# One attention-and-feed-forward kernel: normaliser steps taken from GpSimd to VectorE but for the power, single fillers, token groups of three tiles, and a new order for all engines

## Chip, cores, metric

The kernel runs on one core of one Trainium2 chip, as one program. The metric is the device time of one execution in microseconds (us). A core has five engines with queues of their own that are served in order: TensorE (PE, matmuls), VectorE (DVE), ScalarE (ACT), GpSimd (POOL) and SyncE (SP), which here does nothing but issue DMAs. TensorE runs at one of two clocks, 1.2 or 2.4 GHz; the profile shows which was granted as 0.5 or 1.0.

## What is computed

Three layers, one after the other. First a gated linear attention (2 batches x 8 heads, 768 steps, head size 40), which the reference writes as a recurrence:

```
m_new = max(f + m, i);  f_stab = exp(f + m - m_new);  i_stab = exp(i - m_new)
C = f_stab * C + i_stab * v k^T;   n = f_stab * n + i_stab * k
y = sigmoid(o_gate) * (C q) / max(|n.q|, 1)
```

Its output, 1536 tokens by 320, goes through `rms = sqrt(mean(x*x) + 1e-6); xn = x / rms * rms_g`, then `(silu(xn @ w_gate) * (xn @ w_val)) @ w_out` with 1536 inner columns, then `leaky_relu(x @ w_in, 0.01) @ w_out` with 2048. Everything is float32.

## The kernel before

**Tiles.** The 1536 tokens are 12 tiles of 128 (tile T is chunk T//2 of batch T%2). The attention goes tile by tile: `qk` (scores of q and k), `arg` and `mask` (the exponents), `p` (their product), `av` and `inn` (the output within the chunk and from the state), `kv`, `st`, `cb`, `c` (the state C of that batch, which the tile after next needs), then the normaliser: `abs`, `rec`, `y1`, `yr`, `sq`, `y2`, `xn`, `xc`, and at the end `tp`, `xh`, `xl`, which transpose the tile and write it into X as a high and a low part. All large matmuls take such pairs, so that two or three matmuls stand for one float32 matmul.

**Feed-forward.** `U.g.f.h` is one up projection: 8 matmuls of 128 inner columns f (gate for h = 0, value for h = 1) over the tokens of group g. `T`, `E`, `M`, `S`, `L` make the activation and its two parts (T and S on ScalarE, the others on VectorE), `D` and `DW` project down. For f below 8 the groups are those of `GA`, for the rest those of `GB` (four tiles each). `H`, `R`, `S`, `L`, `O` are the same for the last layer. A U over a group can start when the X of all its tiles is written.

**Weights** come as 64-bit words in chunks (`wA`, `wR`, `wB` load; `a`, `r`, `b` are the four steps that convert one chunk on VectorE and ScalarE; `x` copies part of it into place by DMA).

**Order.** Nothing is scheduled by a tool: the long string `ORDER` (line 41) names every step once, `play` (line 743) issues them in that order, and each engine's queue holds its own steps in that order. An engine whose next step has to wait holds everything behind it. `id.n` (`busy`, line 173) puts n matmuls of constants into TensorE's queue; they depend on nothing and their result is never read. `att_av` adds small ones (128x184) for tiles 0 and 1 by `FILL`.

**The steps that the change touches.** `att_y2` (line 427) turns the sum of squares of a tile into 1/rms: one scale-and-add, a power of -0.5 on 128x1, and three steps of one Newton iteration, all five on GpSimd (lines 431 to 436). GpSimd also adds the mask (`att_mask`, line 310), scales the state and keys (`att_c`, `att_k`) and multiplies `eb` by q (`att_eq`, line 314).

Of the kernel before, what the change touches and what calls it, by code (L numbers as in the profile page):

```python
# [43 lines left out]
cl wA.0 a.0 id.2 dq.0 a.0 a.0 a.0 id.8 ms did dfg dig wB.0 sf.0.1 wR.1 sa.0.1 sf.1.2 sa.1.2 dmk sf.2.6 sa.2.6 eg.2.6  # L44
ex.2.6 uv.0.1 wR.0 ug.2.6 dn.0 ux.2.6 co.0.0.1 cv.0.0.1 fa.0 arg.0.0 r.1 id.2 dA.0.2 ev.1.2 wA.1 a.1 uv.1.2 fa.1
arg.0.1 qk.0 p.0.1 ex.1.2 co.1.2.6 cv.1.2.6 dsl id.2 a.1 ux.0.1 co.1.0.1 cv.1.0.1 th.0 da.2 mask.2.1 k.0 wB.1 mask.2.0
co.0.1.2 p.0.0 ux.1.2 da.1 arg.1.0 r.1 r.1 arg.1.1 a.1 a.1 co.1.1.2 av.0.0 av.0.1 kv.0 r.1 wA.3 b.0 cv.1.1.2 co.0.2.6
b.1 b.0 dr.2.6 b.0 b.0 dE.1.2 dE.2.6 r.0 dq.2 qk.2 dn.2 th.2 cv.0.1.2 dq.1 qk.1 r.0 r.0 dA.2.6 dn.1 k.1 wA.2 abs.0 b.1
arg.2.0 p.2.0 b.1 b.1 da.3 r.0 st.0 k.2 a.2 rec.0 de.2 y1.0 a.2 a.2 dr.1.2 id.9 wR.3 a.3 dn.3 p.1.0 mask.3.1 p.1.1
av.1.0 av.1.1 abs.1 kv.1 th.1 eq.2 arg.2.1 y1.1 id.7 yr.0 sq.0 a.3 rec.1 yr.1 mask.3.0 arg.3.0 x.1 p.2.1 av.2.0 av.2.1  # L50
sq.1 cb.0 dgb y2.0 xn.0 xc.0 a.3 id.2 wR.2 id.2 inn.2 wA.4 y2.1 abs.2 xn.1 xc.1 kv.2 tp.1 arg.3.1 dc.1.2 a.3 st.1 dq.3
qk.3 da.4 a.4 dq.4 y1.2 rec.2 yr.2 sq.2 a.4 y2.2 th.3 tp.0 xh.0 k.3 dv.1.2 a.2 mask.4.1 p.3.0 av.3.0 p.3.1 wB.2 cb.1
av.3.1 de.3 eq.3 cv.0.2.6 mask.4.0 dn.4 k.4 da.5 x.0 c.3 xh.1 xl.1 arg.4.1 mask.5.1 c.2 qk.4 de.4 eq.4 xl.0 a.4 r.2
U.0.1.1 U.0.1.0 T.0.1 E.0.1 M.0.1 a.4 inn.3 kv.3 dq.5 y1.3 dc.2.6 abs.3 arg.4.0 dv.2.6 xn.2 xc.2 U.0.0.0 T.0.0 E.0.0
arg.5.1 tp.2 xh.2 p.4.1 U.0.0.1 wB.3 p.4.0 S.0.1 M.0.0 S.0.0 b.2 st.3 qk.5 da.7 id.1 b.2 b.2 b.2 av.4.0 av.4.1 inn.4
th.4 mask.5.0 arg.5.0 rec.3 mask.7.1 yr.3 sq.3 xl.2 L.0.0 x.3 x.2 dn.5 p.5.1 y1.4 y2.3 id.1 U.0.3.0 T.0.3 E.0.3 c.4
p.5.0 dq.6 xn.3 abs.4 rec.4 yr.4 xc.3 sq.4 y2.4 kv.4 dn.6 k.6 id.2 de.5 L.0.1 U.0.2.0 tp.3 r.2 eq.5 xh.3 cb.3 c.5
T.0.2 b.3 U.0.3.1 M.0.3 qk.6 wA.5 st.4 cb.4 b.3 E.0.2 r.2 b.3 k.5 xn.4 xl.3 xc.4 arg.7.1 U.0.2.1 tp.4 xh.4 S.0.3 dq.7
da.6 av.5.0 av.5.1 inn.5 wB.4 M.0.2 S.0.2 L.0.2 de.6 th.5 xl.4 r.2 abs.5 x.4 a.5 wR.4 kv.5 y1.5 a.5 U.1.1.0 a.5 rec.5
L.0.3 dn.7 b.3 T.1.1 E.1.1 U.1.0.0 T.1.0 E.1.0 mask.6.0 arg.6.0 p.6.0 D.0.0.0 mask.6.1 arg.6.1 p.6.1 th.6 mask.7.0  # L60
arg.7.0 eq.6 U.1.1.1 U.1.0.1 th.7 M.1.0 st.5 K.0.0.0 D.0.0.2 K.0.0.2 wA.7 a.5 b.4 b.4 S.1.0 k.7 da.8 x.5 r.4 L.1.0 r.4
av.6.0 U.1.2.0 mask.8.1 b.4 b.4 c.6 r.3 yr.5 dq.10 av.6.1 wB.6 r.4 r.4 r.3 M.1.1 D.0.0.1 K.0.0.1 inn.6 kv.6 st.6 T.1.2
qk.7 cb.5 c.7 y1.6 U.1.2.1 mask.8.0 sq.5 de.7 y2.5 E.1.2 M.1.2 p.7.0 p.7.1 U.1.3.1 xn.5 eq.7 S.1.2 L.1.2 dn.10 r.3 r.3
S.1.1 arg.8.0 L.1.1 U.1.3.0 T.1.3 E.1.3 M.1.3 S.1.3 av.7.0 dq.8 av.7.1 U.0.5.0 T.0.5 E.0.5 inn.7 U.0.5.1 da.10
mask.10.1 cb.6 abs.7 b.6 dn.8 M.0.5 de.8 arg.10.1 U.0.4.0 L.1.3 D.1.0.1 K.1.0.1 U.0.4.1 S.0.5 k.8 T.0.4 b.6 b.6 b.6
arg.8.1 D.1.0.0 wB.7 mask.10.0 E.0.4 abs.6 M.0.4 wA.6 a.6 y1.7 a.7 qk.8 a.6 a.6 x.6 xc.5 wB.5 kv.7 p.8.1 a.7 eq.8 a.6
D.1.0.2 U.0.6.0 rec.7 yr.7 L.0.5 K.1.0.0 U.0.6.1 T.0.6 rec.6 sq.7 tp.5 st.7 b.7 p.8.0 av.8.0 av.8.1 yr.6 S.0.4 th.8
a.7 E.0.6 M.0.6 sq.6 dn.9 a.7 x.7 U.0.7.0 U.0.7.1 L.0.4 inn.8 kv.8 b.5 xh.5 b.5 y2.7 xn.7 S.0.6 T.0.7 E.0.7 M.0.7
dq.11 S.0.7 L.0.7 b.7 U.1.4.0 T.1.4 E.1.4 arg.10.0 U.1.4.1 xl.5 U.1.5.1 de.10 b.5 b.5 da.9 mask.9.1 b.7 b.7 L.0.6
D.0.1.0 y2.6 xn.6 xc.6 c.8 M.1.4 dq.9 K.0.1.0 S.1.4 L.1.4 tp.6 abs.8 xh.6 xl.6 K.1.0.2 U.1.5.0 T.1.5 E.1.5 da.11  # L70
mask.11.0 D.0.1.2 mask.11.1 xc.7 tp.7 M.1.5 xh.7 U.1.6.0 arg.9.1 qk.9 T.1.6 st.8 de.11 U.1.6.1 D.0.1.1 mask.9.0
arg.9.0 p.9.0 de.9 eq.9 xl.7 k.9 wA.8 p.9.1 S.1.5 av.9.0 L.1.5 E.1.6 K.0.1.2 M.1.6 qk.10 S.1.6 p.10.0 cb.7 c.9 U.1.7.0
T.1.7 E.1.7 K.0.1.1 eq.10 y1.8 U.1.7.1 av.9.1 M.1.7 S.1.7 L.1.7 U.2.2.0 T.2.2 wR.6 U.2.2.1 rec.8 yr.8 av.10.0 p.10.1
av.10.1 sq.8 wR.5 r.5 L.1.6 th.10 y2.8 E.2.2 M.2.2 S.2.2 id.2 U.2.1.0 T.2.1 E.2.1 xn.8 eq.11 inn.9 xc.8 D.1.1.1 wB.8
b.8 b.8 L.2.2 cb.8 D.1.1.0 K.1.1.0 inn.10 y1.10 qk.11 abs.10 rec.10 arg.11.1 arg.11.0 p.11.0 kv.9 st.9 abs.9 rec.9
th.9 y1.9 yr.9 sq.9 yr.10 sq.10 y2.10 U.2.1.1 M.2.1 y2.9 U.2.0.0 T.2.0 tp.8 E.2.0 xh.8 dn.11 U.2.0.1 M.2.0 K.1.1.1
D.1.1.2 K.1.1.2 xn.9 S.2.0 xc.9 p.11.1 U.2.3.0 wA.9 L.2.0 S.2.1 L.2.1 wB.10 av.11.0 av.11.1 cb.9 r.5 r.5 th.11 r.5
U.2.3.1 T.2.3 xl.8 inn.11 E.2.3 M.2.3 S.2.3 abs.11 tp.9 wR.8 L.2.3 D.2.0.0 D.2.0.2 a.8 xn.10 xc.10 K.2.0.0 rec.11
y1.11 yr.11 sq.11 tp.10 y2.11 xh.10 xl.10 D.2.0.1 xn.11 xc.11 tp.11 close U.2.4.0 a.8 a.8 a.8 x.8 xh.11 a.9 a.9 T.2.4
E.2.4 a.9 xl.11 a.9 x.9 U.2.5.0 T.2.5 U.2.5.1 E.2.5 M.2.5 b.8 xh.9 xl.9 S.2.5 L.2.5 U.2.6.0 U.2.6.1 T.2.6 U.2.4.1  # L80
M.2.4 U.2.7.0 S.2.4 L.2.4 U.3.3.1 E.2.6 M.2.6 S.2.6 L.2.6 T.2.7 E.2.7 U.2.7.1 M.2.7 wA.11 a.11 wA.10 K.2.0.2 b.8 S.2.7
r.6 r.6 wR.7 r.6 r.6 U.3.0.0 T.3.0 E.3.0 U.3.0.1 M.3.0 S.3.0 a.10 a.11 a.10 L.2.7 K.2.0.1 U.3.1.0 T.3.1 L.3.0 U.3.3.0
D.2.1.0 K.2.1.0 a.10 a.10 a.11 x.11 a.11 D.2.1.1 b.10 K.2.1.1 U.3.1.1 T.3.3 E.3.3 M.3.3 D.2.1.2 E.3.1 M.3.1 S.3.1 b.10
S.3.3 x.10 wA.12 a.12 b.10 L.3.3 U.3.2.0 T.3.2 a.12 a.12 x.12 L.3.1 wA.15 E.3.2 U.3.2.1 M.3.2 wA.13 a.12 S.3.2 L.3.2
U.3.7.1 b.10 U.3.7.0 a.13 a.13 a.13 a.13 a.15 D.3.0.2 x.13 K.2.1.2 U.3.5.0 T.3.7 E.3.7 M.3.7 S.3.7 L.3.7 wB.9 b.9
D.3.0.1 K.3.0.2 a.15 a.15 a.15 K.3.0.1 wA.17 a.17 T.3.5 E.3.5 a.17 a.17 a.17 U.3.4.0 T.3.4 E.3.4 U.3.4.1 M.3.4 r.8 r.8
r.8 r.8 D.3.0.0 K.3.0.0 U.3.5.1 M.3.5 S.3.5 b.9 U.0.8.0 S.3.4 L.3.4 U.0.8.1 L.3.5 U.0.9.0 U.0.9.1 T.0.8 E.0.8 M.0.8
S.0.8 b.9 b.9 T.0.9 E.0.9 L.0.8 M.0.9 S.0.9 wA.14 a.14 U.0.11.0 U.0.10.0 T.0.10 L.0.9 a.14 a.14 E.0.10 U.0.10.1 M.0.10
# [736 lines left out]
```

## Time and profile before

| | before |
|---|---|
| median of 3 runs | 499.04 us (498.31 to 499.47) |
| profiled execution | 499.9 us, its span 498.1 us |
| TensorE busy | 473.1 us (95%), mean granted clock 0.931 |
| VectorE / ScalarE / GpSimd busy | 275.7 / 223.8 / 76.3 us |
| read from HBM | 43.31 MB |

The span is the time from the first to the last instruction; 1.8 us of the execution lie around it. In the rows further down, a view by windows gives for each stretch the busy time of each engine (with the number of its instructions in brackets), the granted TensorE clock, the mean busy share of the DMA engines and the GB/s moved. A timeline gives start, duration, engine, line, operation, output and inputs, and in square brackets how long the engine was idle before and what released it. Matmuls overlap in their pipeline, so a busy TensorE is not TensorE at its peak, and the start of the next instruction tells more than a duration. Times count from the start of the span.

### The profile page before, as it was taken

To read this page: it belongs to the slowest core of one execution; us is meant where nothing else is said; L and a number is where in the kernel's file an instruction comes from. 1 tells how busy PE (TensorE), PEld (TensorE's weight loads), DVE (VectorE), ACT (ScalarE), POOL (GpSimd) and SP (SyncE) were. 2 spreads that over 40 slices of the span, in tenths; PEclk is the share of its full clock that TensorE was granted. 3 is DMA by queue.
4 is the path that set the end of the run, shared out by engine and by line. 5 is a ranking of instruction groups with operands and counts; after the bars stand their busy time and mean duration, and the time that the engine had idled before them with its cause. 6 is when DMAs were issued, how large, how long until landed. Compare 5 with 4: busy or idle time off the path is not lost.

```text
span 498.1 us, 7422 instructions
## 1 busy us (share of the span) xinstructions
PE 473.1 (95%) x2758; PEld 419.9 (84%) x2764; DVE 275.7 (55%) x570; ACT 223.8 (45%) x525; POOL 76.3 (15%) x130
## 2 busy tenths in 40 slices
...
PEclk8565579699999999999999999999999999999999
...
DMA packets 36868, 51.10 MB, mean 103 GB/s; under 512 B 2800, under 2 KB 26272, under 8 KB 36832
## 3 DMA queue, kind: packets, MB, share of 16 engines
...
q14 instruction: 14, 0.11, 0.1%
HBM read 43.31 MB, written 2.06 MB: 91 GB/s over the span
## 4 chain that ended last, share of the span: by engine, by line
PE 81%; DVE 5%; ACT 3%; DMA 2%; issue 1%; POOL 1%; DVEq 0%; POOLq 0%; ACTq 0%; SPq 0%
PE h L563 18%; PE g L563 12%; PE v L563 12%; PE xa L626 7%; PE oa L698 6%; PE oa L697 6%; PE oa L696 6%; PE o L349 5%; PE xw L644 4%; PE o L360 2%; PE s L284 2%; PE busy L178 1%; PE o L372 1%; DMA raw_A<-wi 1%; ACT w L300 1%
## 5 line engine op out<-in xcount | busy, mean ns | idle before, releaser
L563 PE MATMUL h<-X,wA 128*128 128x512 f32 x384 | 91.1, 390 | 0.0
L608 DVE TENSOR_TENSOR sl<-u,sh 128x512 fp32r<-128x512 f32 x48 | 32.6, 691 | 94.0 <-ACT sh L602 93.9
L563 PEld LDWEIGHTS h<-X,wA 128*128 128x128 f32 x384 | 71.3, 188 | 14.0
L563 PE MATMUL g<-X,wA 128*128 128x512 f32 (+2 forms) x352 | 76.9, 364 | 0.0
L563 PE MATMUL v<-X,wA 128*128 128x512 f32 (+2 forms) x352 | 74.1, 356 | 2.1 <-DVE th L596 1.7
L563 PEld LDWEIGHTS v<-X,wA 128*128 128x128 f32 x352 | 61.0, 191 | 9.5 <-DVE th L596 2.0
L563 PEld LDWEIGHTS g<-X,wA 128*128 128x128 f32 x352 | 63.1, 197 | 7.0
L698 PE MATMUL oa<-wB,sl 128*128 128x320 f32 x192 | 59.5, 310 | 0.0
L697 PE MATMUL oa<-wB,sh 128*128 128x320 f32 x192 | 59.3, 309 | 0.0
L696 PE MATMUL oa<-wB,sh 128*128 128x320 f32 x192 | 59.2, 308 | 0.0
L683 ACT ACTIVATE u<-h 128x512 f32<-128x512 f32 x48 | 28.5, 599 | 61.0 <-PE h L563 54.5
L602 ACT CAST sh<-th 128x512 fp32r<-128x512 f32 (+2 forms) x44 | 23.5, 542 | 51.4 <-DVE th L596 41.4
L626 PE MATMUL xa<-sh,wB 128*128 128x384 f32 (+2 forms) x160 | 45.0, 339 | 0.3 <-DVE x L634 0.3
L349 PEld LDWEIGHTS o<-nat,w 128*128 128x128 f32 x192 | 31.8, 248 | 8.9 <-DVE w L337 6.6
L349 PE MATMUL o<-nat,w 128*128 128x41 f32 x192 | 32.0, 329 | 7.2 <-DVE w L337 5.6
L592 DVE SCALAR_TENSOR_TENSOR th<-th,g 128x512 f32<-128x512 f32 (+2 forms) x44 | 25.8, 587 | 22.7 <-ACT th L585 22.2
L696 PEld LDWEIGHTS oa<-wB,sh 128*128 128x128 f32 x192 | 36.0, 188 | 0.8
L697 PEld LDWEIGHTS oa<-wB,sh 128*128 128x128 f32 x192 | 36.0, 188 | 0.8
L698 PEld LDWEIGHTS oa<-wB,sl 128*128 128x128 f32 x192 | 36.0, 188 | 0.4 <-DVE sl L608 0.4
L602 ACT CAST sh<-u 128x512 fp32r<-128x512 f32 x48 | 29.4, 620 | 11.9 <-PE oa L697 9.9
L608 DVE TENSOR_TENSOR sl<-th,sh 128x512 fp32r<-128x512 f32 (+2 forms) x44 | 26.4, 607 | 13.4 <-ACT sh L602 13.1
L585 ACT ACTIVATE th<-g 128x512 f32<-128x512 f32 (+2 forms) x44 | 22.8, 518 | 23.3 <-PE g L563 17.1
...
## 6 DMA issues: line engine op xcount, KB each, us to landing
...
```

The source lines that it names most:

```text
L349: PE.matmul(num[:, 2 * p + e], t["w"][e][:, p, :], t["vn"][:, 2 * p + e, :], start=(c == 0 or (e == 0 and p == 0)), stop=c == 0,)
L563: PE.matmul(dst, a, x, start=(i == 0), stop=(i == len(seq) - 1))
L585: A.activation(th, u[0], AF.Tanh, scale=0.5)
L592: V.scalar_tensor_tensor(out=u["t"], in0=u["t"], scalar=1.0, in1=u[0], op0=ALU.add, op1=ALU.mult)
L602: A.copy(u["h"], u["t"])
L608: V.tensor_tensor(u["l"], u["t"], u["h"].bitcast(F32), op=ALU.subtract)
L626: PE.matmul(xa, w, x, start=(k == 0), stop=(k == len(seq) - 1))
L644: PE.matmul(xas["w", g, i], a, x, start=(f == NE and k == 0), stop=(f == NF - 1 and k == len(seq) - 1),)
L683: A.activation(t, u[0], AF.Prelu, alpha=0.01)
L696: PE.matmul(dst, sh[:, ts], wb[:, 0:DM], start=first, stop=False)
L697: PE.matmul(dst, sh[:, ts], wb[:, DM:], start=False, stop=False)
L698: PE.matmul(dst, sl[:, ts], wb[:, 0:DM], start=False, stop=last)
```

## The change

Four things change.

1. `att_y2` is cut in three steps. The scale-and-add (step 0) and the Newton iteration (step 2, three instructions) go to VectorE; the power (step 1) stays on GpSimd.
2. `FILL` is 0: the 16 small matmuls of constants in `av.0` and `av.1` are gone. `id` is used singly: there were 40 such matmuls in 13 places, now there are 77, each its own entry; 62 of them stand ahead of the first U (34 before), 8 between `U.0.0.0` and `U.1.0.0`, and 6 among the last stores.
3. `GA` is four groups of three tiles, where it was 2, 3, 3 and 4.
4. `ORDER` is new from the first entry to the last: 1490 entries for 1401. The DMA buffer `A_d` gets a third dimension; its loads and stores are the same.

```
-FILL = 2
+FILL = 0
-GA = ((0, 2), (2, 5), (5, 8), (8, 12))
+GA = ((0, 3), (3, 6), (6, 9), (9, 12))
 ORDER = """
-cl wA.0 a.0 id.2 dq.0 a.0 a.0 a.0 id.8 ms did dfg dig wB.0 sf.0.1 wR.1 sa.0.1 ...
+id.1 dfg id.1 id.1 id.1 ms dig id.1 id.1 sf.0.1 sa.0.1 sf.1.2 sa.1.2 id.1 did ...
...
-    def att_y2(T, E):
+    def att_y2(T, i):
...
+        if i == 0:
+            V.tensor_scalar(out=v_, in0=ss, scalar1=1.0 / DM, scalar2=1e-6, op0=ALU.mult, op1=ALU.add)
+        elif i == 1:
+            G.tensor_tensor(z, v_, mhalf, op=ALU.pow)
+        else:
+            V.tensor_scalar(out=z2, in0=z, scalar1=z, scalar2=v_, op0=ALU.mult, op1=ALU.mult)
+            V.tensor_scalar(out=z2, in0=z2, scalar1=-0.5, scalar2=1.5, op0=ALU.mult, op1=ALU.add)
+            V.tensor_tensor(z, z, z2, op=ALU.mult)
```

Three places of the new order follow. In the names, the number after a name is the tile (or group and f), the last number is the buffer.

**TensorE, about tile 3, before.** `o1` is the output of `av` and `inn`, `v0_1` and `g0_1` the first up projections:

```order
L452 MATMUL tp0_580<-ident_87,xn0_497 128x128 x3
L349 MATMUL o1_3_591<-nat3_413,w3_0_470 128x41 x4
L349 MATMUL o1_3_591<-nat3_413,w3_1_538 128x41 x4
...
L563 MATMUL v0_1_651<-X_93,wA_1_269 128x256 x8
L563 MATMUL g0_1_660<-X_93,wA_1_269 128x256 x8
L360 MATMUL o1_3_591<-Cbd1_99,eb3_605 128x82 x4
```

The same place in the changed kernel (the weight loads of the constants are left out):

```order
L458 MATMUL tp1_647<-ident_87,xn1_592 128x128 x3
L353 MATMUL o1_4_659<-nat4_651,w4_0_653 128x41 x4
...
L182 MATMUL busy_664<-const-bfloat16-1.0 128x512
...
L182 MATMUL busy_676<-const-bfloat16-1.0 128x512
...
L182 MATMUL busy_687<-const-bfloat16-1.0 128x512
L353 MATMUL o1_3_689<-nat3_603,w3_0_525 128x41 x4
L353 MATMUL o1_3_689<-nat3_603,w3_1_566 128x41 x4
...
L182 MATMUL busy_719<-const-bfloat16-1.0 128x512
...
L182 MATMUL busy_723<-const-bfloat16-1.0 128x512
```

No up projection stands here any more; the first one comes after `tp` of tile 2, and fillers stand between the attention's matmuls.

**GpSimd, about the normalisers of tiles 0 and 1, before.** `sm` holds a tile's sums, `Ab` takes the mask, `eb` is multiplied by q:

```order
L310 TENSOR_TENSOR Ab3_378<-Ab3_378,mask_88 128x4x128
L431 TENSOR_SCALAR sm0_364<-sm0_364 128x1
L432 TENSOR_TENSOR sm0_364<-sm0_364,mhalf_90 128x1
L434 TENSOR_SCALAR sm0_364<-sm0_364 128x1
L435 TENSOR_SCALAR sm0_364<-sm0_364 128x1
L436 TENSOR_TENSOR sm0_364<-sm0_364 128x1
L431 TENSOR_SCALAR sm1_435<-sm1_435 128x1
```

In the changed kernel, about the power of tile 1:

```order
L314 TENSOR_TENSOR Ab4_465<-Ab4_465,mask_88 128x4x128
L333 TENSOR_TENSOR Kt1_100<-nat1_291,aeu_93 128x4x40 x2
L314 TENSOR_TENSOR Ab3_519<-Ab3_519,mask_88 128x4x128 x2
L318 TENSOR_TENSOR eb2_415<-eb2_415,qkt2_221 128x512
L438 TENSOR_TENSOR sm1_455<-sm1_455,mhalf_107 128x1
```

The power of tile 1 now stands behind the mask of tiles 4 and 3 and the product of tile 2; four of its neighbours have left the queue.

**VectorE, about the normaliser of tile 1, before:**

```order
L419 TENSOR_TENSOR y1_452<-y1_452,sm1_435 128x320
L337 TENSOR_TENSOR w2_1_447<-s2_1_329,w2_1_447 128x512
L441 SCALAR_TENSOR_TENSOR xn0_497<-y0_392,sm0_364,gb_91 128x320
L441 SCALAR_TENSOR_TENSOR xn1_523<-y1_452,sm1_435,gb_91 128x320
L510 TENSOR_TENSOR wA_3_500<-w32_A3_410,wA_3_500 128x512
```

The same place in the changed kernel:

```order
L208 COPY aeu_93<-pt1_2_506 128x64
L436 TENSOR_SCALAR sm1_455<-sm1_455 128x1
L440 TENSOR_SCALAR sm1_455<-sm1_455 128x1
L441 TENSOR_SCALAR sm1_455<-sm1_455 128x1
L442 TENSOR_TENSOR sm1_455<-sm1_455 128x1
L500 SCALAR_TENSOR_TENSOR w32_A3_494<-raw_A3_492,w32_A3_494 128x512
L525 TENSOR_TENSOR rest_2_532<-w32_R2_462,rest_2_532 128x256
L447 SCALAR_TENSOR_TENSOR xn1_592<-y1_460,sm1_455,gb_90 128x320
```

The four small steps are new in VectorE's queue; between the first and the second of them GpSimd has to do the power.

## Rows read from the trace of the kernel before

**Rows 1.** The page: granted clock in 40 equal slices.

```profile
PEclk8565579699999999999999999999999999999999
```

**Rows 2.** Windows of the span; columns as told above.

```profile
0.00:71.00 71.00, 57.55 (x326) 45.16 (x329) 43.57 (x104) 26.93 (x73) 29.04 (x50) 0.59 0.70 212
71.00:101.00 30.00, 25.57 (x191) 23.55 (x193) 21.25 (x51) 16.25 (x53) 15.13 (x24) 0.83 0.72 220
101.00:195.40 94.40, 91.28 (x710) 88.06 (x710) 64.57 (x148) 50.92 (x154) 32.11 (x56) 1.00 0.43 131
195.40:494.40 299.00, 298.70 (x1538) 263.11 (x1537) 145.44 (x267) 129.70 (x246) 0.00 (x0) 1.00 0.19 55
...
38.40:65.40 27.00, 26.10 (x147) 21.49 (x148) 11.60 (x28) 11.95 (x39) 10.83 (x22) 0.50 0.80 231
...
195.40:249.00 53.60, 53.30 (x258) 46.61 (x258) 39.75 (x77) 26.69 (x55) 0.00 (x0) 1.00 0.46 131
```

**Rows 3.** Two short windows, about the clock's first rise and fall.

```profile
31.75:32.00 0.25, 0.25 (x3) 0.11 (x2) 0.25 (x2) 0.24 (x1) 0.25 (x1) 0.96 0.13 43
35.00:35.25 0.25, 0.00 (x0) 0.00 (x0) 0.25 (x1) 0.00 (x0) 0.25 (x1) 0.87 0.00 0
```

**Rows 4.** Timeline of TensorE: start, duration, work; two sets in the last row.

```profile
30.76 2.19 PE L178 MATMUL busy<-const-bfloat16-1.0 128*128 128x512 bf16 x7 [0.22 <-issue]
38.38 1.08 PE L349 MATMUL o<-nat,w 128*128 128x41 f32 x4 [5.44 <-DVE w L337]
...
45.58 1.91 PE L178 MATMUL busy<-const-bfloat16-1.0 128*128 128x512 bf16 x4 [0.22 <-issue]
47.28 3.48 PE L349 MATMUL o<-nat,w 128*128 128x41 f32 x16
...
65.37 2.07 PE L563 MATMUL v<-X,wA 128*128 128x256 f32 x8
...
70.99 1.21 PE L563 MATMUL g<-X,wA 128*128 128x256 f32 x8
...
95.98 4.90 PE L563 MATMUL g<-X,wA 128*128 128x384 f32 x16
```

**Rows 5.** Chain that ended last, 105 to 140 us: start, us, what.

```profile
108.31 0.82 PE o L349 x8
...
110.64 0.86 PE o L360 x8
111.49 0.59 PE o L372 x13
112.08 1.09 PE s L284 x16
...
116.15 1.39 PE g L563 x8
```

**Rows 6.** Timeline of GpSimd: the five steps of one normaliser, one mask.

```profile
46.10 0.19 POOL L431 TENSOR_SCALAR sm<-sm 128x1 f32<-128x1 f32 x1 [10.33 <-ACT junk L425]
46.38 0.91 POOL L432 TENSOR_TENSOR sm<-sm,mhalf 128x1 f32<-128x1 f32 x1
47.39 0.34 POOL L434 TENSOR_SCALAR sm<-sm 128x1 f32<-128x1 f32 x1
...
48.09 0.19 POOL L436 TENSOR_TENSOR sm<-sm 128x1 f32<-128x1 f32 x1
...
60.88 1.27 POOL L310 TENSOR_TENSOR Ab<-Ab,mask 128x512 f32<-128x512 f32 x1
```

**Rows 7.** Timeline of VectorE.

```profile
34.81 1.24 DVE L490 TENSOR_SCALAR w_A<-raw_A 128x512 uint32<-128x512 uint32 x1
35.98 0.16 DVE L413 TENSOR_SCALAR sm<-sm 128x8 f32<-128x8 f32 x1
...
37.32 0.41 DVE L490 TENSOR_SCALAR w_A<-raw_A 128x512 uint32<-128x512 uint32 x1
```

**Rows 8.** Waits of 0 to 100 us: total, times, longest.

```profile
DVE xn L441 <- POOL sm L436: 2.6, 2, 1.7
```

More of the change, by code (lines that the diff above doesn't have):

```diff
@@ L43 @@
 ORDER = """
[L44 to L88, printed above, removed]
@@ new lines @@
+mask.2.1 arg.2.1 p.1.1 k.2 r.1 id.1 dr.2.6 r.1 cb.0 a.0 dgb av.1.0 av.1.1 de.2 dE.2.6 wA.1 x.0 a.1 mask.2.0 a.2 xn.0
+xc.0 a.1 a.1 x.1 id.1 dq.4 cv.0.2.6 a.2 id.1 tp.0 arg.2.0 abs.1 a.1 wR.2 y1.1 r.2 da.4 mask.4.0 id.1 id.1 rec.1 yr.1
+a.2 wR.3 sq.1 id.1 a.2 r.2 xh.0 id.1 id.1 k.1 wA.3 a.3 kv.1 st.1 co.1.2.6 p.2.0 id.1 av.2.0 da.3 de.3 mask.3.0 arg.3.0
+dq.3 r.2 p.2.1 av.2.1 xl.0 qk.3 cb.1 mask.3.1 id.1 eq.2 inn.2 cv.1.2.6 id.1 id.1 arg.3.1 wR.4 id.1 y2.1.0 y2.1.1
+y2.1.2 a.3 r.2 a.3 id.1 x.2 id.1 id.1 xn.1 mask.4.1 wA.4 a.4 p.3.1 y1.2 dn.3 k.3 p.3.0 id.1 a.3 arg.4.1 abs.2 rec.2
@@ new lines @@
+qk.4 x.3 kv.2 id.1 de.4 eq.4 xc.1 tp.1 dn.4 arg.4.0 p.4.0 av.4.0 id.1 c.3 c.2 r.3 a.4 a.4 yr.2 eq.3 id.1 wA.5 da.5
+mask.5.0 r.3 de.5 id.1 av.3.0 av.3.1 a.4 sq.2 y2.2.0 th.4 p.4.1 y2.2.1 r.3 dn.5 r.3 a.5 y2.2.2 xn.2 xc.2 id.1 mask.5.1
+xh.1 id.1 id.1 inn.3 th.3 a.5 wR.5 abs.3 id.1 kv.3 y1.3 id.1 id.1 xl.1 tp.2 xh.2 xl.2 arg.5.0 id.1 dq.5 wA.6 qk.5
+rec.3 yr.3 a.5 a.5 U.0.0.0 arg.5.1 b.0 a.6 eq.5 st.3 cb.3 p.5.0 p.5.1 k.5 T.0.0 E.0.0 sq.3 da.6 mask.6.1 dc.2.6 dv.2.6
+b.0 a.6 b.0 b.0 U.0.0.1 av.4.1 dq.6 inn.4 a.6 abs.4 wB.1 av.5.0 mask.6.0 arg.6.0 c.5 y2.3.0 y2.3.1 qk.6 y2.3.2 U.0.1.0
@@ new lines @@
+T.0.1 y1.4 M.0.0 rec.4 yr.4 sq.4 dn.7 b.1 av.5.1 a.6 c.4 arg.6.1 k.4 kv.4 xn.3 id.1 xc.3 b.1 id.1 y2.4.0 y2.4.1 inn.5
+kv.5 abs.5 x.6 wA.7 a.7 th.5 st.4 p.6.1 E.0.1 de.6 st.5 da.7 id.1 p.6.0 mask.7.0 wB.3 tp.3 xh.3 xl.3 S.0.0 dn.6 de.7
+dq.7 wB.2 y1.5 U.0.1.1 U.0.2.0 a.7 b.1 L.0.0 a.7 a.7 mask.7.1 arg.7.1 eq.6 av.6.0 id.1 dq.8 av.6.1 rec.5 yr.5 sq.5 b.3
+b.1 b.2 arg.7.0 T.0.2 y2.5.0 dn.10 b.3 id.1 id.1 id.1 b.3 M.0.1 y2.5.1 y2.4.2 xn.4 xc.4 y2.5.2 xn.5 xc.5 x.5 E.0.2 b.3
+da.8 da.9 qk.7 id.1 p.7.0 U.0.2.1 S.0.1 L.0.1 tp.5 xh.5 xl.5 cb.4 th.7 c.6 wA.8 p.7.1 U.0.3.0 T.0.3 E.0.3 M.0.2 inn.6
```

110 lines of the change are left out of this document (69 added, 41 removed).

## The prediction

> **What bounds the kernel now.** I read the granted clock by slices first [rows 1], then the span in windows [rows 2], then TensorE's timeline of the first 100 us [rows 3, 4], and last the chain for prices at full clock [rows 5]. From 101 us on the clock is full; TensorE is busy for 91.28 of 94.4 us up to the last attention transpose, for 298.70 of the next 299.0, and 3.7 us of stores end the span [rows 2]. In those 397 us an order can only give back a few us. The first 101 us are another matter: TensorE is busy for 83 of them but mostly at half clock, VectorE for 65, the DMA engines for about 0.7 of the time [rows 2]. No engine is full. From 38.4 to 65.4 us TensorE is busy for 26.10 of 27.0 us at a granted clock of 0.50, while VectorE works 11.60 [rows 2]: there a half-speed TensorE is the bound. Ahead of it TensorE waits 5.44 us for VectorE [rows 4]. The clock rose at 31.8 us, in a row of seven fillers, and fell at 35.2 us in that wait [rows 3, 4].
>
> So I measure both orders to one mark: the end of `U.1.0.0`, the first up projection of the second group. Before, it ends with the pair of sets at 95.98 + 4.90 = 100.9 us [rows 4]; from there to the end are 397.2 us of the 498.1.
>
> **Groups of three.** The token groups hold the same 12 tiles in four groups, so the number of matmuls and their columns stay. A set of three tiles takes 1.39 us at full clock [rows 5]; four of them cost what 2 + 3 + 3 + 4 cost, by columns. I cost it at nothing by itself. The first U needs three tiles in X where it needed two.
>
> **What lies ahead of the mark.** Counted at the prices of rows 5 (set of three 1.39, scores of a tile 1.09, half of `av` 0.82, `inn` 0.86, `kv` 0.59), the changed order has more useful TensorE work ahead of the mark. Nine sets of three tiles are 12.5 us; before there were eight of two tiles and two of three, 27 tiles in place of 22, so 2.3 us more are done. Two more score tiles are 2.2, two more `av` halves 1.6, one `inn` 0.9, one transpose some 0.4. Together 7.3 us are done earlier. The rest behind the mark is then 397.2 - 7.3 = 389.9 us, if the losses there stay. **Break-even is a mark at 498.1 - 389.9 = 108.2 us.**
>
> **From the start to the first U (`U.0.0.0`).** TensorE's own work there is six score tiles 6.5, nine `av` halves 7.4, two `inn` 1.7, four `kv` 2.4, and three for the transposes and first products (an estimate by their columns): 21 us at full clock. Then the 62 fillers. Four of them took from 45.58 to 47.28 us at half clock, 0.425 each [rows 4]; at full clock I halve it. So 21 + 13 = 34 us at full clock, 68 at half, where `av` indeed takes 3.48 us for two halves [rows 4]. VectorE was busy 43.57 us up to 71 us [rows 2]. Up to `U.0.0.0` the changed order gives it four more steps on A chunks, seven on R chunks, eight fewer on B chunks, two more `p`, one more `xl` and three normalisers: about 5 us more, 48.6 busy, 53 with the start, when nothing has landed. So the first U starts between about 57 us (VectorE with some waits) and 74 (half clock throughout plus 6 us in which TensorE has nothing). I take 67, nearer the half clock: of the two stretches that are alike, one rose behind a row of fillers and one of 27 us never did [rows 2, 3]. Before, the matching set started at 70.99, behind a first one at 65.37 [rows 4].
>
> **From there to the mark.** The same stretch took 30 us (71 to 101), with TensorE busy for 25.57, VectorE for 21.25, at a mean clock of 0.83 [rows 2]. The changed order puts more into it: 8 sets of three, 5 `av` halves, three `inn`, three transposes, 8 fillers, some 25 us at full clock and 50 at half; and 21 conversion steps for 11, so that VectorE has about 1.4 times its work, 30.6 us. At the old pace that would be 42 us; with VectorE full, 31. I take 35, since the conversions stand close behind each other in its queue and GpSimd holds it up less. The mark comes at 67 + 35 = 102 us, 6 us ahead of break-even.
>
> **The normaliser.** Five GpSimd steps took from 46.10 to 48.28 us, the power 0.91 of it [rows 6]. Four move to VectorE, where such a step takes 0.16 us [rows 7]; with the gap to the next I take 0.2: 12 tiles x 4 x 0.2 = 9.6 us of VectorE, of which six tiles, some 5 us, lie ahead of the mark and are in the sums above. GpSimd loses 12 x 1.3 = 15 us. The tile's own chain gets some 0.5 us shorter. The wait that is added: VectorE's queue now stands at the Newton steps until the power is done, with conversions and `p` behind them, for which ScalarE and TensorE wait. Before, it waited 2.6 us in two waits for GpSimd's result [rows 8]. Five of the 12 have nothing between their steps on VectorE, so 5 x 0.91 = 4.6 us of idle, two of them ahead of the mark; the power of tile 1 can also queue behind three 1.27 us steps [rows 6]. So this part is worth between those 2.6 us gained and some 6 lost ahead of the mark; I take it as even.
>
> VectorE's conversion of a chunk took 1.24 us while GpSimd's mask ran, and 0.41 with GpSimd idle [rows 7]. The Trainium skill ("SBUF — State Buffer", section "Who interferes with whom") says why: some VectorE instructions need a port pair that GpSimd also uses, and whichever comes first holds it for its whole instruction. The trace agrees with that row. By that rule three of the four moved steps, being of the one-source kind, may wait too; what that would give is in rival (b). The sum takes none of it, since no row shows a small step held by a mask.
>
> **Behind the mark.** From the last transpose to the first wide up projection VectorE was busy 39.75 of 53.6 us [rows 2]. In the changed order the same VectorE work stands beside some 43.5 us of TensorE work, because more of it was done earlier. That is tight; I add 1.5 us, between 0 and 4. The stores at the end and the six fillers among them cost nothing, since TensorE is done there.
>
> **Sum.** 102 + 389.9 + 1.5 = 493.4 us of span, 4.7 less than 498.1. The profiled execution took 499.9 with 1.8 around its span, and the median of the runs is 0.9 under it; I carry the 4.7 over to the median: 499.0 - 4.7 = **494.3 us**.
>
> **Rivals.**
> (a) The fillers cost more than they give: they stand in ones to sevens between the attention's matmuls, the clock stays at half, and TensorE alone needs 74 us to the first U and some 43 more to the mark. Mark 117, span 508, time 509: slower. For it speaks the stretch from 38.4 to 65.4 us with its ten fillers [rows 2]; against it the rise at 31.8 us behind seven [rows 3, 4]. It decides from a mark later than 108.2. It need not be whole: half of it gives 501.
> (b) VectorE in place of TensorE. Six tiles ahead of the mark bring 18 small scale-and-add steps; if GpSimd's masks hold each as they held the conversion, by 1.24 - 0.41 = 0.83 us [rows 7], that is 15 us at most. A third to a half of it, with the waits for the power, puts the mark at 107 to 110 and the time at 498 to 502. For it speaks VectorE's share, 65 of 101 us already [rows 2]; against it that GpSimd itself works 44 of those 101 us [rows 2] and less after. (The rule of the page on SBUF is this one.)
> (c) The fillers do hold the clock up: first U at 60, mark at 92, time 484. Against it speaks the DMA share of 0.7 to 0.8 in the first 65 us [rows 2]: more weight chunks are loaded ahead of the mark, and that cannot go much faster.
> (d) That the new order changes nothing that counts, since 397 of 498 us are TensorE at full clock, is part of (b).
>
> **Chances.** Forecast (490 to 498) 0.45, (c) 0.14, (b) 0.15, (a) 0.26. About 0.2%, 1 us, is what can be told from no change. Of (b) two thirds fall within that and the rest on the slow side. Faster 0.59, same 0.10, slower 0.31. The range leaves out the lower half of (c) and the upper half of (a): 486 to 505. By itself the forecast holds 490 to 498.
>
> **What would show it.** In the profile of the changed kernel: the first U starts at about 67 us (74 if (a)), the pair with `U.1.0.0` ends at about 102; the granted clock is up in part of the first 65 us; VectorE shows waits for line 438 of GpSimd of about 1 us each, and `w_A` conversions of 1.2 us become rarer; from the mark on TensorE is busy without a break except for a few us. The prediction is wrong if the mark is late although the clock is up (then VectorE or a DMA holds it), or if the mark is early and the time is not, which would put the loss behind the mark.

## The result

The changed kernel takes 490.82 us (median of 4 runs, 489.97 to 492.73), the kernel before 499.25 beside it (498.31 to 499.74): ratio 0.984, 95% interval 0.980 to 0.987. It is 8.4 us faster; 494.3 was predicted, in 486 to 505. The profiled execution took 489.97 us, its span is 488.2. Here and below, the profiled executions of experiments 2 and 5 were disturbed ones and are not read, and one such execution each of 5 and 10 is left out of their ranges.

The page's rows for the granted clock and the DMA engines, 40 slices of 12.2 us (the first answers [rows 1]):

```profile
PEclk7975869999999999999999999999999999999999
DMA  7899996963910011736430410232000000010101
```

The windows that answer to [rows 2]; the cuts are the start of the first U, the mark, the last attention transpose and the end of TensorE's work:

```profile
0.00:65.30 65.30, 51.09 (x350) 35.05 (x350) 48.85 (x121) 30.91 (x84) 29.62 (x41) 0.76 0.95 290
65.30:97.00 31.70, 30.47 (x238) 27.58 (x237) 26.62 (x72) 20.47 (x63) 13.45 (x18) 0.95 0.86 228
97.00:190.90 93.90, 92.18 (x646) 88.81 (x645) 64.60 (x158) 46.24 (x136) 19.73 (x23) 1.00 0.31 87
190.90:484.50 293.60, 293.59 (x1552) 263.14 (x1552) 141.52 (x266) 127.32 (x245) 0.00 (x0) 1.00 0.19 55
```

TensorE's timeline, answering to [rows 4]: `U.0.0.0` is the row at 65.27, `U.1.0.0` the first half of the pair at 95.53.

```profile
60.22 1.08 PE L376 MATMUL o<-nat,Kt 128*64 128x41 f32 x16 [3.96 <-ACT sm L403]
...
65.27 2.93 PE L569 MATMUL g<-X,wA 128*128 128x384 f32 x8
...
68.66 1.67 PE L569 MATMUL v<-X,wA 128*128 128x384 f32 x8
...
95.53 2.94 PE L569 MATMUL g<-X,wA 128*128 128x384 f32 x16
```

So the first set of three tiles starts at 65.27 us, 5.7 us ahead of the matching set before [rows 4], and the mark (the end of `U.1.0.0`) comes at 97.0, where it was 100.9. Behind it 391.2 us remain, where 397.2 did. The 9.9 us between the two spans are these two: 3.9 us to the mark and 6.0 behind it, where less work is left. (They are of one execution each; the medians differ by 8.4.) In the first 65 us the DMA engines are now busy 0.95 of the time, not 0.70 [rows 2].

One reason why they are fuller stands in the waits of the DMA queue (SP) over the first 100 us: by whom it was held, in all, how often, longest. Before, the load of `Ab` (line 270), which waits until ScalarE is done with one of two buffers, held all loads behind it:

```profile
SPq L270 <- ACT w L300: 31.4, 4, 12.8
```

In the changed order the same load (line 274) comes later:

```profile
SPq L274 <- ACT w L304: 4.8, 3, 3.0
```

Other loads wait more than they did, so that all of SP's waits in this stretch still come to some 49 us where they were 62; but the longest is 7.5 us instead of 12.8.

### The profile page after: what moved, and what is told of

The parts are those of the page before. It is cut to its first block, busy times and chain, and to the rows that moved or that the text cites. A ratio compares the mean times of both kernels' runs of the same rounds, so it can differ in the third digit from the quotient of the medians.

```text
span 488.2 us, 7459 instructions
## 1 busy us (share of the span) xinstructions
PE 468.6 (96%) x2785; PEld 415.0 (85%) x2785; DVE 282.5 (58%) x618; ACT 224.9 (46%) x525; POOL 62.8 (13%) x82
## 4 chain that ended last, share of the span: by engine, by line
PE 79%; DVE 8%; DMA 5%; issue 3%; ACT 2%; POOL 1%; SPq 1%; POOLq 0%; DVEq 0%; ACTq 0%
PE h L569 18%; PE g L569 13%; PE v L569 12%; PE xa L632 7%; PE oa L704 6%; PE oa L702 6%; PE oa L703 6%; PE xw L650 4%; PE o L353 2%; DMA Ab<-A_d 2%; DMA raw_A<-wgv 2%; PE s L288 1%; PE o L364 1%; DMA wA<-rest 1%; PE o L376 1%
## 5 line engine op out<-in xcount | busy, mean ns | idle before, releaser
L569 PE MATMUL h<-X,wA 128*128 128x512 f32 x384 | 93.0, 395 | 0.0
L569 PE MATMUL g<-X,wA 128*128 128x384 f32 (+1 forms) x352 | 75.0, 359 | 0.0
L569 PE MATMUL v<-X,wA 128*128 128x384 f32 (+1 forms) x352 | 74.1, 356 | 0.6 <-DVE th L602 0.6
L632 PE MATMUL xa<-sh,wB 128*128 128x384 f32 x160 | 46.2, 339 | 0.0
L608 ACT CAST sh<-th 128x384 fp32r<-128x384 f32 (+1 forms) x44 | 23.6, 541 | 46.8 <-DVE th L602 39.3
L591 ACT ACTIVATE th<-g 128x384 f32<-128x384 f32 (+1 forms) x44 | 22.7, 518 | 27.6 <-PE g L569 20.3
L598 DVE SCALAR_TENSOR_TENSOR th<-th,g 128x384 f32<-128x384 f32 (+1 forms) x44 | 25.7, 587 | 14.8 <-ACT th L591 14.2
L614 DVE TENSOR_TENSOR sl<-th,sh 128x384 fp32r<-128x384 f32 (+1 forms) x44 | 27.0, 617 | 12.2 <-ACT sh L608 11.9
L632 PE MATMUL xa<-sl,wB 128*128 128x384 f32 x96 | 32.4, 338 | 0.0
L182 PE MATMUL busy<-const-bfloat16-1.0 128*128 128x512 bf16 x77 | 27.6, 477 | 4.1 <-DVE aeu L208 3.4
```

The source lines that it names most:

```text
L182: PE.matmul(dst, idle[0], idle[1][:, 0:dst.shape[1]], start=start, stop=start)
L569: PE.matmul(dst, a, x, start=(i == 0), stop=(i == len(seq) - 1))
L591: A.activation(th, u[0], AF.Tanh, scale=0.5)
L598: V.scalar_tensor_tensor(out=u["t"], in0=u["t"], scalar=1.0, in1=u[0], op0=ALU.add, op1=ALU.mult)
L608: A.copy(u["h"], u["t"])
L614: V.tensor_tensor(u["l"], u["t"], u["h"].bitcast(F32), op=ALU.subtract)
```

## Experiments

All times are medians of 4 to 12 runs; "ratio" is against runs of the kernel before on the same chip (500.16 us beside experiments 1 to 4, 499.59 beside 5 to 8, 500.03 beside 9 to 12). First a table of what the profiles show. "First U" is the first up projection of the order; in the old order that is `U.0.1.1`, and `U.0.0.0` comes some 5 us later (70.99 before). Mark and rest are worked out as above, from the span and the pair with `U.1.0.0` (in the old order its second half). The last four columns are of one execution each, and the two of the changed kernel differ by 3.2 us at the first U and by 4.0 at the mark: a difference of that size between two rows of these columns shows nothing by itself.

| kernel | median us (range) | ratio, 95% interval | profiled us | first U | mark | rest of the span |
|---|---|---|---|---|---|---|
| before | 499.25 (498.31-499.74) | 1 | 499.9 | 65.4 | 100.9 | 397.2 |
| changed | 490.82 (489.97-492.73) | 0.984 (0.980-0.987) | 489.97 | 65.3 | 97.0 | 391.2 |
| 12 changed, again | 489.45 (486.96-494.11) | 0.980 (0.975-0.984) | 494.11 | 68.5 | 101.0 | 391.3 |
| 1 changed, no fillers | 491.21 (488.52-493.37) | 0.983 (0.980-0.987) | 488.52 | 62.6 | 95.1 | 391.6 |
| 2 changed, groups 2 3 3 4 | 497.65 (493.18-504.55) | 0.994 (0.991-0.997) | - | - | - | - |
| 8 changed, groups 3 2 3 4 | 496.72 (492.52-499.32) | 0.994 (0.991-0.997) | 492.96 | 63.6 | 95.5 | 395.7 |
| 3 changed, steps on GpSimd | 491.74 (487.04-495.93) | 0.982 (0.977-0.986) | 490.35 | 67.0 | 97.6 | 390.9 |
| 4 changed, wait removed | 489.48 (487.48-491.58) | 0.979 (0.975-0.983) | 488.97 | 62.6 | 96.0 | 391.2 |
| 5 changed, 2.1 MB more | 496.18 (493.36-496.51) | 0.993 (0.990-0.995) | - | - | - | - |
| 9 as 4, a chunk later | 488.02 (486.83-489.85) | 0.976 (0.974-0.979) | 487.64 | 61.7 | 92.8 | 393.1 |
| 10 as 9, no fillers | 490.86 (489.51-491.92) | 0.981 (0.978-0.984) | 491.92 | 62.4 | 94.7 | 395.4 |
| 6 before, 2.1 MB more | 497.06 (491.94-499.50) | 0.994 (0.991-0.997) | 493.9 | 55.5 | 95.1 | 397.0 |
| 7 before, no fillers | 495.55 (493.40-499.71) | 0.993 (0.990-0.996) | 495.38 | 61.5 | 96.9 | 396.7 |
| 11 before, steps on VectorE | 511.21 (508.91-515.34) | 1.025 (1.021-1.029) | 508.91 | 64.6 | 102.2 | 404.9 |

The last column is the steadiest: 390.9 to 391.6 for five profiles of the new order with groups of three. Run to run, the changed kernel varies ahead of the mark (97.0 and 101.0), not behind it.

**1. Without fillers.** The 70 `id.1` ahead of `U.1.0.0` are left out.

```
-id.1 dfg id.1 id.1 id.1 ms dig id.1 id.1 sf.0.1 ...
+dfg ms dig sf.0.1 ...
```

> The changed kernel without the 70 fillers that stand ahead of U.1.0.0 (the 6 among the last stores stay). Filler theory: they hold TensorE's clock up (granted 0.76 up to the first U, 0.59 before), so without them the granted clock up to the first U falls to 0.6 or less, the mark (end of U.1.0.0, 97.0 us in the changed kernel) comes 5 us later or more, and the time goes to 496 us or above. Order theory (mine): the first 65 us are bound by loads and by VectorE, the fillers matter for 1 to 3 us either way: 489 to 494 us. Rival (a) of the prediction, fillers in the way of useful work: faster than the changed kernel, 485 to 489 us.

Measured: 491.21, no difference from the changed kernel. The filler theory falls, and rival (a) with it: in this order the fillers neither win nor cost anything that can be told. The clock shows why, once it is read from durations. The window from 24 to 65 us, and three rows of TensorE (its lines stand two lower in this kernel):

```profile
24.00:65.00 41.00, 33.73 (x208) 30.80 (x208) 33.20 (x69) 22.96 (x68) 23.61 (x25) 1.00 1.02 296
```

```profile
24.33 2.08 PE L286 MATMUL s<-qkt 40*128 40x128 f32 x16
...
62.60 2.93 PE L567 MATMUL g<-X,wA 128*128 128x384 f32 x8
...
65.87 1.66 PE L567 MATMUL v<-X,wA 128*128 128x384 f32 x8
```

The granted clock reads 1.00, but the 16 score matmuls take 2.08 us and the first set 2.93, about twice the 1.09 and 1.39 of [rows 5], and the set behind it 1.66: TensorE ran at half clock up to 65 us. Even so its first U comes at 62.6 us, no later than with the fillers. In the new order TensorE's clock is not what the first U waits for; the DMA engines are busy all the time (1.02), VectorE for 33.20 of the 41 us.

**2 and 8. The old groups.** The new order as it is, with token groups of 2, 3, 3, 4 tiles, and of 3, 2, 3, 4.

```
-GA = ((0, 3), (3, 6), (6, 9), (9, 12))
+GA = ((0, 2), (2, 5), (5, 8), (8, 12))      # experiment 2
+GA = ((0, 3), (3, 5), (5, 8), (8, 12))      # experiment 8
```

> The changed kernel with the token groups of before, 2, 3, 3 and 4 tiles; order and all else as changed. By the prediction groups of three are worth nothing by themselves: the time stays within 1.5 us of the changed kernel's 490.8 us. The rival, that equal groups are a part of the gain, expects 493 us or more: the first set is of two tiles, so 27 tiles ahead of the mark become 4 x 2 + 5 x ... fewer, and each set of four tiles keeps its VectorE steps longer.

> The changed kernel with groups of 3, 2, 3 and 4 tiles: the first group stays at three, the third and fourth are those of before. With 2, 3, 3 and 4 it took 497.65 us for 490.8. If what counts is the first group (eight sets of three tiles in place of two ahead of the mark, 0.44 us more of useful work each, and a TensorE that is busy enough for the full clock from 68 us): 490 to 492.5 us. If what counts is the group of four tiles, with its longer activation steps and its later start: 495 us or more.

Measured: 497.65 and 496.72. Both lose 6 to 7 us of the 8.4, and a first group of three doesn't save it. In the profile of experiment 8 the mark is as early as ever, and the loss lies behind it (rest 395.7 for 391.2; 0.4 of it is the smaller `U.1.0.0`). From its mark to the end of TensorE's work, in experiment 8:

```profile
95.50:487.40 391.90, 388.25 (x2196) 345.39 (x2197) 206.69 (x424) 173.78 (x380) 19.71 (x24) 1.00 0.21 62
```

TensorE is idle for 3.65 us of it. In the changed kernel, from 97.00 to 484.50, it is idle for 1.73 (the last two windows of the result). What TensorE waits for in experiment 8, 97 to 192 us:

```profile
PE v L569 <- DVE th L598: 1.3, 4, 0.4
...
PE g L569 <- DVE th L598: 0.4, 1, 0.4
```

The changed kernel has no such waits for line 598 (the activation's step `E`), while VectorE's work behind the mark is the same (206.69 us here, 206.1 there). A set of two tiles gives TensorE 0.95 us (in the chain of the kernel before, at full clock) where one of three gives 1.39 [rows 5], and the conversions and attention steps that stand beside it in VectorE's queue are the same. The waits are shown, for 1.7 of about 4 us; that the shorter sets cause them is argued. The rest of the 4, and the 3.8 us by which this kernel's median lies above its profiled execution, stay open. Groups of three with the old order were not run: that order starts its sets before tiles 2 and 5 are in X.

**3. The steps back on GpSimd.** In the new order, steps 0 and 2 of `att_y2` on GpSimd.

```
-            V.tensor_scalar(out=v_, in0=ss, ...
+            G.tensor_scalar(out=v_, in0=ss, ...
```

> The changed kernel with the four small normaliser steps back on GpSimd; order as changed. The prediction cost the move at nothing (between 2.6 us gained and 6 lost). If the move is even: within 1.5 us of 490.8 us. If it is a part of the gain: 493 us or more, with waits of VectorE for GpSimd's line 442 of several us. If the waits for the power cost more than the steps gave: 489 us or less, and VectorE's waits of 3.3 us for the power become shorter.

Measured: 491.74, even. In this order the move is worth nothing, as it was cost.

**11. The steps on VectorE, in the old order.** The kernel before with this part alone.

```
-y2.0 xn.0 ...
+y2.0.0 y2.0.1 y2.0.2 xn.0 ...
```

> The kernel before with one part of the change alone: the scale-and-add and the Newton steps of all 12 normalisers on VectorE, the power on GpSimd, at the old places of the order. The part was cost at nothing, and in the new order putting the steps back on GpSimd gave 491.7 us for 490.8: within 1.5 us of 499.5. If VectorE's waits for the power hold the conversions behind them in the old order: 502 us or more.

Measured: 511.21, 11.2 us slower than the kernel before beside it (500.03). In the profiles the mark is only 1.3 us later; 7.7 us are lost behind it (rest 404.9 for 397.2). Waits of TensorE there, in its timeline:

```profile
117.37 1.66 PE L567 MATMUL v<-X,wA 128*128 128x384 f32 x8 [1.27 <-DVE th L596]
...
150.19 0.52 PE L456 MATMUL tp<-ident,xn 128*128 128x128 f32 x3 [1.19 <-DVE xn L445]
...
187.51 2.93 PE L567 MATMUL v<-X,wA 128*128 128x384 f32 x8 [4.08 <-DVE sm L434]
```

and VectorE's waits for the power, 97 to 200 us:

```profile
DVE sm L438 <- POOL sm L436: 4.7, 6, 1.3
```

TensorE's waits between the mark and the last transpose add up to 9.0 us, where they were 3.0, and behind the longest of them it is at half clock (2.93 for a set). Ahead of that one VectorE stood 0.88 us for the sum of squares and 0.67 for the power, with the activation's step (line 600) behind them. In the kernel before it was GpSimd that did the waiting, for the sum of squares (0 to 110 us):

```profile
POOL sm L431 <- ACT junk L425: 19.6, 3, 10.3
```

At the same places of the order VectorE now stands, with the activation's steps behind it. In the changed kernel, 97 to 192 us, the waits for the power are less than half of that:

```profile
DVE sm L440 <- POOL sm L438: 2.1, 3, 0.7
```

So the half of rival (b) that is about waits for the power is real, and the new order is what keeps it small.

**4. The wait at 60 us.** In the changed kernel the power of tile 2 stands behind a mask that waits for its transfer; the chain of waits (start, us, what):

```profile
37.73 8.01 DMA raw_A<-wgv
45.82 9.07 DMA Ab<-A_d
55.05 1.22 POOL Ab L314
56.52 0.74 POOL sm L438
57.78 0.72 DVE sm L442
58.53 0.56 DVE xn L447
60.22 1.08 PE o L376 x12
```

```
-... eq.3 id.1 wA.5 da.5 mask.5.0 r.3 ... a.5 y2.2.2 xn.2 xc.2 id.1 mask.5.1 xh.1 id.1 id.1 inn.3 th.3 a.5 wR.5 abs.3 id.1 kv.3
+... eq.3 id.1 wA.5 da.5 r.3 ... a.5 mask.5.0 inn.3 abs.3 kv.3 y2.2.2 xn.2 xc.2 id.1 mask.5.1 xh.1 id.1 id.1 th.3 a.5 wR.5 id.1
-... da.3 de.3 mask.3.0 arg.3.0 ... mask.3.1 ... wR.4 id.1 y2.1.0 y2.1.1 y2.1.2
+... da.3 de.3 y2.1.0 y2.1.1 mask.3.0 arg.3.0 ... mask.3.1 ... wR.4 id.1 y2.1.2
```

The last two lines are a second move, which the expectation does not name: the scale-and-add and the power of tile 1 go ahead of the masks of tile 3.

> The changed kernel with five entries moved: the mask of tile 5 behind the power of tile 2 in GpSimd's queue, and inn, abs and kv of tile 3 ahead of the Newton steps and xn of tile 2. In the changed kernel the power of tile 2 stands behind a mask that waits for a transfer until 55.05 us, and TensorE is idle for 3.96 us ahead of 60.22 because ScalarE's abs of tile 3 stands behind the same tile's normaliser. If that wait is on the path: first U 2 to 4 us earlier than 65.27 and 487 to 489 us. If the first 65 us are bound by the transfers (DMA engines 0.95 busy) all the same: the first U moves less than 1 us and the time stays at 490 to 491.5 us.

Measured: 489.48. TensorE's wait fell from 3.96 to 0.60 us and VectorE's waits for the power almost went, here in the changed kernel and in experiment 4 (0 to 100 us):

```profile
DVE sm L440 <- POOL sm L438: 3.9, 2, 3.3
```

```profile
DVE sm L440 <- POOL sm L438: 0.7, 1, 0.7
```

The first U came 2.7 us earlier, as the first theory expects, but the mark only 1.0 us, and the time can't be told from the changed kernel's (490.82 and 489.45), as the second expects. Inconclusive between the two: what the first U gained is within what it varies by, and most of it is gone by the mark.

**5 and 6. More transfers.** Four transfers of 512 KB that nobody reads, in the changed kernel and in the one before.

```
+    def extra(i):
+        d = dram.tile([128, 1024], U32, name=f"extra{i}")
+        Q.dma_start(out=d, in_=wgv[11].bitcast(U32))
```

> The changed kernel with four more transfers of 512 KB (HBM to HBM, read by nobody) in SP's queue, behind the loads wA.1, wR.2, wR.3 and wA.3, so some 15 to 40 us into the span. If the transfers bound the stretch up to the first U (DMA engines 0.95 busy at 290 GB/s, and a run without fillers, at half clock, did not come later): 2.1 MB more at 290 GB/s are 7 us, the first U starts at 70 to 72 us and the time is 495 to 498 us. If VectorE or TensorE bounds it: less than 2 us, up to 492.5 us.

> The kernel before with the same four transfers, behind wA.1, wB.1, wA.3 and wA.2. Its DMA engines are busy 0.70 of the first 71 us, with 20 us free. If the order of before is not bound by transfers but by what stands behind a waiting entry in SP's queue and by TensorE at half clock: within 2 us of 499.3. If transfers bound it too: 504 us or more.

Measured: 496.18 for the changed kernel, 5.4 us more (4 to 6.5 by the ratios to the kernel before): near the 7 of the transfer theory, above the 2 of the other. That the loss lies ahead of the first U was not seen, for want of a profile that can be read. The kernel before got no slower but slightly faster, 497.06. Its window from 24 to 65 us, the wait of its TensorE for `w`, and its first U:

```profile
24.00:65.00 41.00, 35.14 (x266) 27.13 (x265) 24.97 (x65) 21.66 (x69) 20.86 (x34) 0.74 0.83 250
```

```profile
36.11 0.64 PE L349 MATMUL o<-nat,w 128*128 128x41 f32 x4 [0.76 <-DVE w L337]
...
55.48 2.08 PE L567 MATMUL v<-X,wA 128*128 128x256 f32 x8
```

The same window of the kernel before without them:

```profile
24.00:65.00 41.00, 34.44 (x209) 27.66 (x212) 23.55 (x54) 18.60 (x57) 16.59 (x28) 0.54 0.73 211
```

In that execution the clock was up for half of the window, and the first U came 10 us earlier in spite of 2.1 MB more. So before, the bound of this stretch was TensorE at half clock, and transfers had room; after, more transfers cost time. That the transfers alone are the bound there is not shown: no run took load away without taking VectorE's conversions away too. Why the clock stayed up in experiment 6 is open; the wait of 5.44 us in which it fell before [rows 3, 4] was one of 0.76 there.

**7. Before, without its fillers.** `FILL = 0`, and no `id` ahead of `U.1.0.0`.

> The kernel before without its fillers ahead of U.1.0.0 (38 of 512 columns) and without the 16 small ones in av of tiles 0 and 1. If TensorE at half clock bounds the stretch from 38 to 65 us, as the prediction had it, the fillers that stand there (ten, and the small ones) only take its time: 3 to 6 us faster, 493 to 496. If they do nothing for or against, as in the changed kernel: within 1.5 us of 499.3. If they hold the clock up somewhere: 502 us or more.

Measured: 495.55, 4 us faster, as the theory of the half clock expects. Three rows of TensorE:

```profile
38.58 3.64 PE L349 MATMUL o<-nat,w 128*128 128x41 f32 x16 [9.43 <-DVE w L337]
...
53.09 2.08 PE L284 MATMUL s<-qkt 40*128 40x128 f32 x16
...
61.52 2.07 PE L563 MATMUL v<-X,wA 128*128 128x256 f32 x8
```

Half clock still (2.08 for the scores), no fillers in the way, first U 3.9 us earlier and mark 4.0. `av` of tile 1 starts at 38.58, as it did before (38.38 [rows 4]): all of it is won from there on, where the fillers stood. In the old order the fillers cost about what they occupied. Half of the change's gain was to be had by leaving them out.

**9 and 10. A chunk later.** The order of experiment 4, with A chunks 5 and 6 one place later and chunk 7 behind the mark; and the same without fillers.

```
-... wA.5 ... wA.6 ... U.0.0.0 ... x.6 wA.7 a.7 ... wA.8 ... wA.10 ... U.1.0.0
+... wA.5 ... U.0.0.0 ... wA.6 a.6 ... wA.7 ... wA.8 ... U.1.0.0 ... a.7 x.7 wA.10
```

> The order of the run with inn, abs and kv of tile 3 moved ahead (489.5 us), and besides every A chunk from the sixth on one place later: chunk 5 where chunk 6 stood, 6 where 7 stood, 7 behind the mark. So 0.5 MB less is loaded and one chunk less is converted ahead of the first U and ahead of the mark. If transfers bound these 97 us: 0.5 MB at 290 GB/s, 1.8 us, 487 to 488.5 us, first U at 60.5 to 61.5. If the chunk was free there, or is missed later: 489 to 491 us.

> The same without the 70 fillers ahead of U.1.0.0. In the changed kernel they were worth nothing: 491.2 us without, 490.8 with. If TensorE is not the bound of the first 65 us even at half clock, this one is within 1.5 us of the same order with fillers. If the earlier loads bring TensorE to the bound, 2 us slower or more.

Measured: 488.02 and 490.86. The first is the fastest kernel of the study (2.4% under before). Its mark comes at 92.8 us, 3.2 us ahead of experiment 4's; behind it 1.9 are given back. Against the changed kernel run beside it, 489.45, the intervals overlap, so the version is likely but not surely better. As a chunk less is loaded and also a chunk less converted ahead of the mark, it does not tell the transfers from VectorE. Without fillers it is 2.8 us slower, as the second theory expects: its mark comes 1.9 us later and 2.3 more are lost behind it. TensorE's clock shows much of it. A set that takes 1.64 us in experiment 4 takes this in experiment 9:

```profile
111.54 2.86 PE L570 MATMUL g<-X,wA 128*128 128x384 f32 x8
```

and in experiment 10 there are two such stretches at half clock, each behind a wait:

```profile
83.81 2.93 PE L567 MATMUL v<-X,wA 128*128 128x384 f32 x8 [1.60 <-DVE th L600]
...
113.02 2.00 PE L362 MATMUL o<-Cbd,eb 104*128 104x82 f32 x8 [0.91 <-POOL eb L316]
114.75 2.91 PE L567 MATMUL g<-X,wA 128*128 128x384 f32 x8
```

With less to load, TensorE's clock counts again. That leaving out the fillers costs the 2.8 us is shown; why the clock falls behind the mark, in experiment 9 with no wait ahead of it, is not.

**12. The changed kernel again.**

> The changed kernel itself, beside the others on the same chip: 489 to 492 us, 0.980 to 0.987 of before.

Measured: 489.45, as expected. Its profiled execution was the slowest of the six, and all of it lies ahead of the mark (101.0).

## Why the prediction was right, and where not

The time fell inside the forecast, but the change gained 8.4 us where 4.7 were expected. Of its four parts the fillers and the normaliser's move are worth nothing in the new order; the order with groups of three is what gains, and with the old groups the same order keeps only 2.5 to 2.9 us.

**The bound before**: right. From 38 to 65 us it was TensorE at half clock, as experiments 6 and 7 show from two sides.

**Start to the first U**, 67 us taken, 65.3 measured, 68.5 in another execution: right in size, for a reason that fails. The step took the time "nearer the half clock" because TensorE would still be the bound. It isn't: without fillers, at half clock throughout, the first U comes at 62.6, and more transfers move the time. VectorE's sum was right: 48.6 us counted, 48.85 measured. The step saw the DMA share of 0.7 to 0.8 and used it only against rival (c). It didn't count the transfers as it counted TensorE: the new order moves 18.9 MB ahead of its first U (290 GB/s for 65.3 us), the old one 15.1 (212 GB/s for 71), and at the old rate with a full share, 212 / 0.70 = 303 GB/s, 18.9 MB would take 62 us by themselves (an estimate).

**First U to the mark**, 35 us taken, 31.7 measured (30.6 to 32.5 in experiments 1, 3 and 12): the mis-sized term. It came out near the lower of its own bounds, 31 with VectorE full, but not for that reason: VectorE is busy 26.62 of 31.70 us and TensorE 30.47, at a mean clock of 0.95 where the old stretch had 0.83 [rows 2]. So the bound is a TensorE at nearly full clock, which the step had only as its 25 us of work. VectorE's 30.6 us were too many: they rest on 21 conversion steps for 11, and the old order has 14 there (eight `b`, three `r`, three `a`). This and the 1.7 us of the term before make up the 5 us by which the mark came earlier than 102.

**Behind the mark**, 389.9 + 1.5 = 391.4 us taken, 391.2 measured, and 390.9 to 391.6 in four more profiles: right as a sum, in part by luck. (The five terms of the work done earlier add up to 7.4, not 7.3.) The 1.5 us were for a VectorE too tight behind the last transpose; TensorE lost nothing there, being busy for 293.59 of 293.60 us. From the mark to that transpose it was idle for 1.7 us where it had been for 3.1 [rows 2], while the step took those losses as they were. What made up for most of both stands in no term: the 384 matmuls of the last layer's up projections got slower. The page's row before, and in the changed kernel (busy us, mean ns):

```profile
L563 PE MATMUL h<-X,wA 128*128 128x512 f32 x384 | 91.1, 390 | 0.0
```

```profile
L569 PE MATMUL h<-X,wA 128*128 128x512 f32 x384 | 93.0, 395 | 0.0
```

These 1.9 us stand in every profile read of the new order and in none of the old one; why is open. The count of useful work ahead of the mark is the step that made the forecast hold, to about 2 us; that the sum met to 0.2 is chance.

**Groups of three**, cost at nothing by themselves: wrong. Undone in the new order they cost 6 to 7 us. The columns are the same, as the step says; what it left out are TensorE's waits for VectorE behind shorter sets, shown for 1.7 us of it.

**The normaliser**, cost as even: right in the new order (experiment 3), and wrong as a price of the move by itself: in the old order it costs 11 us (experiment 11). The range, up to 6 us lost, was for the waits ahead of the mark, where 1.3 were lost; the dear ones lie behind it. That the power of tile 1 would queue behind three steps came true. GpSimd's queue:

```profile
38.99 2.50 POOL L314 TENSOR_TENSOR Ab<-Ab,mask 128x512 f32<-128x512 f32 x2 [2.29 <-DMA Ab<-A_d]
41.44 1.27 POOL L318 TENSOR_TENSOR eb<-eb,qkt 128x512 f32<-128x512 f32 x1
42.66 0.56 POOL L438 TENSOR_TENSOR sm<-sm,mhalf 128x1 f32<-128x1 f32 x1
43.18 1.27 POOL L314 TENSOR_TENSOR Ab<-Ab,mask 128x512 f32<-128x512 f32 x1
```

and VectorE's, where the wait for it is 3.28 us (it answers to [rows 8]); the last row is of a normaliser beside which GpSimd has nothing to do:

```profile
39.83 0.15 DVE L436 TENSOR_SCALAR sm<-sm 128x1 f32<-128x1 f32 x1
43.26 0.27 DVE L440 TENSOR_SCALAR sm<-sm 128x1 f32<-128x1 f32 x1 [3.28 <-POOL sm L438]
43.56 0.15 DVE L441 TENSOR_SCALAR sm<-sm 128x1 f32<-128x1 f32 x1
43.75 0.72 DVE L442 TENSOR_TENSOR sm<-sm 128x1 f32<-128x1 f32 x1
...
87.29 0.16 DVE L442 TENSOR_TENSOR sm<-sm 128x1 f32<-128x1 f32 x1
```

In experiment 4, where these waits fell from 3.9 to 0.7 us, the time gained nothing that can be told: ahead of the first U they cost little.

**Rival (b)** had the wrong steps held. Beside the mask at 43.18 the two one-source steps took 0.27 and 0.15, no more than elsewhere; the one with two sources took 0.72 for 0.16. The Trainium skill ("SBUF — State Buffer", section "Who interferes with whom") also says that an instruction of VectorE with two SBUF inputs contends with a GpSimd instruction that reads SBUF; the trace agrees, and at 0.6 us for some of 12 tiles it is far from the 15 us of the rival. **Rivals (a) and (c)** both fall with experiment 1. The first half of (c) is true: with fillers the clock is up for part of the first 65 us (mean 0.76), without them it is not; but the first U does not come earlier for it.
